# An attention-and-feed-forward kernel whose whole work becomes a list of jobs, planned into one fixed order for all five engines

## The chip, the cores and the metric

The kernel runs on one core of a Trainium2 chip. That core has a matrix engine (PE; its weight loads are listed apart as PEld), a vector engine (DVE), an activation engine (ACT), a general engine (POOL), a queue engine (SP) that issues most transfers, and 16 DMA engines that carry them out. Each engine works through its own list of instructions strictly in order, and waits at the head of that list when an operand is not there yet. The metric is the device time of one execution in microseconds (us); lower is better.

## The reference: what is computed

There are 4 batches of 8 heads with 768 rows of 64 elements. Rows may only attend to rows that fall in the same of 64 hash buckets. The attention output, with the heads side by side, is 3072 rows of 512, and goes through a feed-forward stage with 2048 hidden units and an ELU. All inputs are float32.

```
q_bits = (einsum('bhsd,dk->bhsk', q, proj) > 0);  k_bits likewise      # 6 bits each
mask   = bucket(q_bits)[:, :, :, None] == bucket(k_bits)[:, :, None, :]
scores = where(mask, (q @ k.T) / sqrt(64), -1e9)
attn   = exp(scores - max(scores));  attn = attn / (sum(attn) + 1e-9)
x      = (attn @ v) with heads side by side                             # (3072, 512)
h      = x @ w_in                                                        # (3072, 2048)
g      = where(h > 0, h, exp(min(h, 0)) - 1)
out    = g @ w_out                                                       # (3072, 512)
```

## The kernel before, in words

**Numbers.** Every float32 operand of a matrix product is split into a high and a low half-precision part after scaling by a power of two. ACT writes the high part (a scaled copy, `scaled`, L142), DVE the low part (`rest`, L151, a scalar_tensor_tensor). A product is then three products: high by high, high by low, low by high.

**Weights.** The 16 tiles of `w_in` and the 16 of `w_out` are loaded 512 KB at a time (L503), taken apart on ACT and DVE (`wdecode`, L516 to L518), and PE forms bounds of their size (L526). From these come one scale for `w_in` (`w0s`) and one for `w_out` (`w1s`), after which every tile is split in place (`wsplit`; the rows `W<-W,w0s` and `W<-W,w1s`). The ring that the raw weights land in is the same memory (`U`) that the feed-forward stage later uses for its intermediate results, so that stage begins only when all 32 tiles are decoded.

**Attention.** A pair is two heads and half of a batch's rows (384 rows per head). Each pair has six slots, one for 128 rows of one head against all 768 keys. There are 32 pairs and 192 slots. In a slot PE makes the scores (`s`, L556, four matmuls), DVE clamps them and takes the row maximum (L568, `pt<-s`), ACT takes the exponential with its sum (L584), ACT and DVE write the normalized result as two halves (`hl`), and SP issues a transposing transfer (`PT<-hl`, L599). After its sixth slot a pair's product with v runs on PE (`attend`, `av`, 36 matmuls, L607) and ACT and DVE split its result into `x`. Before a pair's slots its q and k rows are loaded, scaled, split, transposed by a transfer, and their hash bits are written beside them (`z`, L315; `zb`, L320). Each batch's v is prepared likewise.

**Feed-forward.** A chunk is the 384 rows of four pairs; there are eight. For each of 16 groups of hidden units, `first` makes `h` (12 matmuls, L636), then ACT takes the exponential (L647), POOL scales and shifts (L650), DVE combines (L651), ACT and DVE split (`U<-U,ch`), and `second` adds into the output banks `o` (9 matmuls, L672). After a chunk's last group the banks are scaled out by ACT or DVE and sent from POOL's queue (`out_dram<-W`, L686).

**What sets the order.** The program is written as a loop over slots `G`. Tables of leads in slots (`PREP`, `VPREP`, `MOE_LAGS`, `AV_LAG`) say ahead of or behind which slot each step is written, and `run_moe` writes feed-forward work between the slots in a proportion that finishes a chunk's feed-forward while the next chunk's slots run. From the slot at which the first chunk's attention is done on, PE's list is exactly as written (`tc.manual_schedule` for PE alone). On the other engines, and on PE before that slot, the framework's own scheduler sets the order by its estimate of when each instruction can run.

## Time and profile before

| what | value |
|---|---|
| median of 3 runs | 922.37 us (921.95 to 925.62) |
| the profiled execution's own time | 921.71 us |
| its span, first to last instruction | 919.9 us |
| PE busy | 824.0 us, 90% of the span |
| DVE busy | 701.2 us, 76% |
| ACT busy | 696.8 us, 76% |
| POOL busy | 127.1 us, 14% |
| mean granted clock of PE | 0.945 |

The shares are means over stages that differ. The first feed-forward matmul starts 165 us into the span. Until then the work is weights, preparation and attention; afterwards attention and feed-forward run side by side, and at the end there is feed-forward alone. A row of the profile names the line and the engine, the tile written and the tiles read, and the shapes; `x128` is a count, a busy time is followed by the mean duration of one in nanoseconds, and an idle time stands with what ended it.

### The profile page before, as it was taken

The numbers are of one execution on the slowest core, as the hardware profiler recorded it, in microseconds if no ns is written. First come the engines' busy times: TensorE is split into PE (matmuls) and PEld (weight loads), VectorE is DVE, ScalarE is ACT, GpSimd is POOL, SyncE is SP. The second block draws the span as 40 slices with busy tenths as digits, with TensorE's granted clock in tenths as the row PEclk, the third lists the DMA queues.
The fourth block names the chain that finished last, engine by engine and source line by source line (L and its number), as shares of the span: only waits on it lengthen the run. The fifth ranks groups of instructions, "written<-read, shape, count | busy, mean of one in ns | idle before, by whom it ended". The sixth has DMA issues, their size and how long they took to land.

```text
span 919.9 us, 14869 instructions
## 1 busy us (share of the span) xinstructions
PE 824.0 (90%) x5161; PEld 441.4 (48%) x5161; DVE 701.2 (76%) x1530; ACT 696.8 (76%) x1361; POOL 127.1 (14%) x179
## 2 busy tenths in 40 slices
PE   4566456999999999999999999999999999999996
PEld 2334223455545555555445555555445555555553
DVE  6999899788877777789968686889777687674332
ACT  7877889879879677888878686888687777774332
POOL 1000000011121011221111011121111012111211
PEclk9586576899999999999999999999999999999999
DMA  9798668699887857798897777886966667654000
GB/s 325 213 259 245 170 128 156 131 172 174 164 185 149 149 104 152 149 192 134 165 200 131 130 132 130 168 177 118 168 138 130 113 117 150 99 107 81 35 1 35
DMA packets 391339, 135.12 MB, mean 147 GB/s; under 512 B 368000, under 2 KB 385632, under 8 KB 391264
## 3 DMA queue, kind: packets, MB, share of 16 engines
q1 hardware_dynamic: 389184, 127.88, 69.2%
q0 software_dynamic: 1920, 6.29, 2.0%
q8 instruction: 40, 0.66, 0.3%
q14 instruction: 35, 0.29, 0.1%
q10 hardware_dynamic: 160, 0.00, 0.0%
HBM read 35.65 MB, written 6.29 MB: 46 GB/s over the span
## 4 chain that ended last, share of the span: by engine, by line
PE 41%; DVE 18%; DMA 17%; ACT 14%; issue 8%; POOL 1%; SPq 1%; POOLq 0%; DVEq 0%; ACTq 0%
PE h L636 14%; PE o L672 14%; PE s L556 6%; PE av L607 6%; DVE pt L568 5%; DMA K<-natk 4%; DVE hl L151 4%; ACT pt L584 4%; DMA O<-nat1q 3%; ACT hl L142 3%; DMA out_dram<-W 2%; DMA PT<-hl 2%; DVE vhl L151 1%; ACT U L647 1%; POOL U L650 1%
## 5 line engine op out<-in xcount | busy, mean ns | idle before, releaser
L672 PE MATMUL o<-W,U 128*128 128x512 f16 x1152 | 279.5, 379 | 3.9 <-ACT W L142 3.9
L636 PE MATMUL h<-x,W 128*128 128x384 f16 x1536 | 280.5, 327 | 2.1 <-ACT x L616 1.8
L650 POOL TENSOR_SCALAR U<-U,ch 128x384 f32<-128x384 f32 x128 | 110.3, 862 | 750.8 <-ACT U L647 511.7
L636 PEld LDWEIGHTS <-W 128*128 128x128 f16 x1536 | 147.6, 98 | 113.9 <-issue 13.1
L584 ACT ACTIVATE pt<-pt,nb,sg 128x768 f32<-128x768 f32 x192 | 195.3, 1019 | 2.2
L151 DVE SCALAR_TENSOR_TENSOR hl<-pt,r,hl 128x768 f16<-128x768 f32 x192 | 189.0, 1011 | 7.0 <-ACT hl L142 6.7
L142 ACT ACTIVATE hl<-pt,r 128x768 f16<-128x768 f32 x192 | 168.3, 924 | 23.5 <-DVE r L594 22.4
L568 DVE TENSOR_SCALAR_CACHE_REDUCE pt<-s 128x768 f32<-128x768 f32 x177 | 168.2, 950 | 21.1 <-PE s L556 20.7
L556 PE MATMUL s<-K,O 128*128 128x384 f16 x708 | 151.3, 336 | 22.5 <-DVE pt L568 20.0
L672 PEld LDWEIGHTS <-U 128*128 128x128 f16 x1152 | 110.7, 97 | 122.8 <-issue 8.5
L651 DVE SCALAR_TENSOR_TENSOR U<-h,U 128x384 f32<-128x384 f32 x128 | 70.9, 554 | 74.9 <-POOL U L650 74.9
L556 PEld LDWEIGHTS <-O 128*128 128x128 f16 (+1 forms) x768 | 74.5, 102 | 108.1 <-issue 54.7
L647 ACT ACTIVATE U<-h,ch 128x384 f32<-128x384 f32 x128 | 72.8, 569 | 65.9 <-PE h L636 65.8
L607 PE MATMUL av<-PT,vhl 128*64 128x384 f16 x1152 | 109.5, 341 | 8.4 <-DMA PT<-hl 3.9
L151 DVE SCALAR_TENSOR_TENSOR U<-U,ch 128x384 f16<-128x384 f32 x128 | 79.6, 623 | 41.2 <-ACT U L142 40.9
L142 ACT ACTIVATE U<-U,ch 128x384 f16<-128x384 f32 x128 | 77.2, 605 | 41.6 <-DVE U L651 41.4
L607 PEld LDWEIGHTS <-vhl 128*64 128x64 f16 x1152 | 75.1, 114 | 45.4 <-issue 20.7
L581 ACT ACTIVATE nb<-m,sg 128x2 f32<-128x2 f32 x96 | 27.6, 288 | 18.1 <-DVE pt L568 17.8
L584 ACT ACTIVATION_READ_ACCUMULATOR pt<-pt,nb,sg 128x1 f32 x192 | 36.0, 188 | 0.0
L208 ACT ACTIVATE nat1q<-qst 128x384 bf16<-128x384 f32 x30 | 15.4, 514 | 21.9 <-DMA O<-nat1q 20.6
L594 DVE RECIPROCAL r<-r 128x2 f32<-128x2 f32 x96 | 15.2, 159 | 19.1 <-ACT r L593 19.1
L556 PE MATMUL so<-K,O 128*128 128x384 f16 (+1 forms) x60 | 19.2, 454 | 10.0 <-DVE pt L568 9.2
(123 smaller groups left out, 583.6 us busy)
## 6 DMA issues: line engine op xcount, KB each, us to landing
U<-in_moe_w_in_dram SPq DMA_DIRECT2D x12, 512.0 KB
vf<-in_v_dram SPq DMA_DIRECT2D x16, 384.0 KB
U<-in_moe_w_out_dram SPq DMA_DIRECT2D x12, 512.0 KB
out_dram<-W POOLq DMA_DIRECT2D x24, 256.0 KB, 3.2
qst<-in_q_dram SPq DMA_DIRECT2D x30, 192.0 KB
kst<-in_k_dram SPq DMA_DIRECT2D x14, 384.0 KB
PT<-hl SPq DMA_TRANSPOSE x192
W<-in_moe_w_in_dram SPq DMA_DIRECT2D x4, 512.0 KB
```

Of the source, the lines that this page charges most:

```text
L142: nc.scalar.activation(o, x, AF.Copy, scale=s)
L151: nc.vector.scalar_tensor_tensor(o, x, s, hi, ALU.mult, ALU.subtract)
L556: nc.tensor.matmul(s_tile[:, n, :HALF], st[o][:rows, at, :], kst[kk][:rows, j * NC + n * HC : j * NC + (n + 1) * HC, :].rearrange("p a b - ...
L568: top = nc.vector.tensor_scalar(pt.rearrange("p (n e) -> p n e", n=2), s_tile[:, :, :HALF], CLAMP, None, ALU.max, ALU.max, accum_out=duo[0 ...
L581: nc.scalar.activation(nb[:, :w], m[:, :w], AF.Copy, scale=st["sg"][:, 1:2])
L584: nc.scalar.activation(pt, pt, AF.Exp, bias=nb[:, n : n + 1], scale=st["sg"][:, 0:1], accum_out=sm[:, n : n + 1])
L607: nc.tensor.matmul(av[j * D : (j + 1) * D], vt[:, j, c, vx, :], PTs[j][:, :, px, c, :], start=n == 0, stop=n == last,)
L636: nc.tensor.matmul(h, WH[:, g * KT + t, wx, fc * P : (fc + 1) * P], c["xs"][t][:, xx, :], start=n == 0, stop=n == 3 * KT - 1,)
L647: nc.scalar.activation(e, h, AF.Exp, scale=c["ch"])
L650: nc.gpsimd.tensor_scalar(e, e, c["up"], c["dn"], ALU.mult, ALU.add)
L651: nc.vector.scalar_tensor_tensor(e, h, 0.0, e, ALU.max, ALU.min)
L672: nc.tensor.matmul(o[t][:, :DO], g16[:, gx, t * P : (t + 1) * P], WH[:, NSI + 1 + f, wx, :], start=f == 0 and i == 0, stop=f == NF - 1 and ...
```

## The change

All of the work is now written down as jobs. A job names its engine, an assumed duration, a function that emits its instructions, a key, the jobs that it comes after, and tokens that it takes and gives back (one for each buffer of a ring: score banks, `PT` tiles, `x` tiles and so on). The jobs stand for the same operations on the same tiles as before: each engine's list has the same operations in the same numbers, apart from a few one-column scalings that are now made once for each batch and not once for each chunk. Nothing about tiles, buffers, shapes or transfers is altered.

`run_plan` then goes through time in its own reckoning. At each step it looks, on every engine, for the jobs whose predecessors are done and whose tokens are free, takes the one that could start first (among those within `EAGER` of it, the one with the smallest key), emits it, and books its end. Keys of attention count slot pairs; keys of feed-forward matmuls start at 1000, so that on PE attention goes ahead of feed-forward whenever both could start. On ACT, DVE and POOL the feed-forward steps have negative keys and go ahead of attention. A job may not be taken while its key is more than `AHEAD` past the furthest attention slot. The order in which the jobs were taken is the order that all five engines now get (`tc.manual_schedule` for PE, ACT, DVE, POOL and SP). The tables of leads and the framework's scheduling are gone.

```diff
-FIRST = [3, 3]
-OTHER = (3, 3)
-MOE_LAGS = (6, 6, 6)
-AV_LAG = 4
-PREP = (18, 14, 10, 5)
...
+MULTI = 1.5
+EAGER = 0.05
+AHEAD = 6.0
+HOP = 0.06
+LATE = {"PE": 0.17, "ACT": 0.1, "DVE": 0.09, "POOL": 0.1, "SP": 0.0}
+LEAD = (6.0, 5.0, 4.0, 3.0)
+W_KEY = (-1.0, 0.35, 1.0, 4.0, 0.3, 12.0, 0.5)
+S_LAG = 5
+OUT = ("ACT", "DVE", "ACT")
...
+    def run_plan():
...
+            for u, js in near.items():
+                opts = []
+                for j in js:
+                    t = max(free[u], j.ready)
+                    ok = j.key <= front + AHEAD or j.key >= 1000
+                    for name in j.take:
+                        if not tokens[name]:
+                            ok = False
+                            break
+                        t = max(t, min(tokens[name]))
+                    if ok:
+                        opts.append((t, j))
...
+                t0 = min(t for t, _ in opts)
+                t, j = min((x for x in opts if x[0] <= t0 + EAGER), key=lambda x: (x[1].key, x[0]))
+                if best is None or t < best[0]:
+                    best = (t, j)
...
+            j.start = t
+            free[j.unit] = t + us
+            j.end = t + us + LATE[j.unit]
+            if j.move is not None:
+                dma = max(dma, t + 0.1) + j.move
+                j.end = max(j.end, dma) + 1.5
+            for name in j.give:
+                tokens[name].append(j.end)
+            j.do()
...
+                s = job("PE", 0.66, scores, D0 + d + OFF["S"], after=kst["ready"] + st["ready"], behind=(last_scores,),
+                        take=(which,), give=give)
...
+            parts.append(job("PE", 1.05, attend, ka, after=landed + list(vst["ready"][p]), behind=parts[-1:],
+                             take=("av",) if n_ == 0 else (),
...
+                prev = job("PE", 0.49, first, 1000 + 2 * seq, after=[qs[n]["x"] for n in ns] + [w_ready[g * KT + t]],
+                           behind=(prev,), take=("h",) if t == 0 else (), give=give)
...
+                prev = job("PE", 0.65, second, 1000 + 2 * seq + S_LAG, after=after, behind=(prev,), give=("g",) if t == HC - 1 else ())
...
+    with tc.manual_schedule(engines={E_.PE, E_.Activation, E_.DVE, E_.Pool, E_.SP}):
+        run_plan()
```

The first place where the order can be seen is ACT's list around the first exponential of the feed-forward stage (the row `U<-h,ch`). `W<-W,w1s` is the high part of a `w_out` tile, `hl` that of a normalized slot, `pt` an exponential, `duo` or `nb`, `r` the small columns beside it, `nat1q` and `natk` the work on q rows and on k or v rows. Before:

```order
L142 ACTIVATE W<-W,w1s 128x512
L208 ACTIVATE nat1q,qx<-qst 128x384
L142 ACTIVATE hl<-pt,r 128x768 x2
L581 ACTIVATE nb<-m,sg 128x2
L142 ACTIVATE W<-W,w1s 128x512
L584 ACTIVATE pt,sm<-pt,nb,sg 128x768 x2
L616 ACTIVATE x_1529<-av 128x384
L208 ACTIVATE nat1q,qx<-qst 128x384
L142 ACTIVATE W<-W,w1s 128x512
L593 ACTIVATE r<-sm 128x2
L647 ACTIVATE U<-h,ch 128x384
```

With the change:

```order
L205 ACTIVATE W<-W,w1s 128x512
L205 ACTIVATE hl<-pt,duo 128x768
L239 ACTIVATE natk,vx<-vf 128x768
L205 ACTIVATE hl<-pt,duo 128x768
L929 ACTIVATE U<-h,ch 128x384
L239 ACTIVATE natk,kx<-kst 128x768
L785 ACTIVATE duo<-duo,sg 128x2
L239 ACTIVATE natk,kx<-kst 128x768
L792 ACTIVATE pt,duo<-pt,duo,sg 128x768
L205 ACTIVATE U<-U,ch 128x384
L929 ACTIVATE U<-h,ch 128x384
L792 ACTIVATE pt,duo<-pt,duo,sg 128x768
```

Before, 15 of the 16 `w_out` tiles are split ahead of the first feed-forward row; now 7 are, and nine come later. Of the squares of k rows six stood ahead of it, the first batch's four and two of the next batch; now the first batch's four do.

The second place is DVE's list between the 16th and the 17th feed-forward group (`U<-h,U` is one row for each group). `pt<-s` or `pt,duo<-ss` is the maximum of one attention slot. Before:

```order
L617 SCALAR_TENSOR_TENSOR x_2760<-av,x_2760 128x384
L568 TENSOR_SCALAR pt,m<-s 128x768
L693 SCALAR_TENSOR_TENSOR ch<-ve,w0e 128x1
L694 SCALAR_TENSOR_TENSOR ch<-vs,w0s 128x1
L151 SCALAR_TENSOR_TENSOR hl<-pt,r,hl 128x768 x2
L695 RECIPROCAL ch<-ch 128x1
L697 TENSOR_TENSOR ch<-ch 128x1
L568 TENSOR_SCALAR pt,m<-s 128x768
L696 TENSOR_SCALAR ch<-ch 128x1
L651 SCALAR_TENSOR_TENSOR U<-h,U 128x384
L568 TENSOR_SCALAR pt,m<-s 128x768
L151 SCALAR_TENSOR_TENSOR U<-U,ch 128x384
```

With the change:

```order
L805 RECIPROCAL duo<-duo 128x2
L769 TENSOR_SCALAR pt,duo<-ss 128x768
L402 COPY K_2606<-K_2605 64x1536
L208 SCALAR_TENSOR_TENSOR natk<-kst,ks,natk 128x12x64
L208 SCALAR_TENSOR_TENSOR hl<-pt,duo,hl 128x768
L514 COPY nat1q<-nat1q 128x6x64
L769 TENSOR_SCALAR pt,duo<-ss 128x768
L208 SCALAR_TENSOR_TENSOR hl<-pt,duo,hl 128x768
L208 SCALAR_TENSOR_TENSOR nat2q<-qst,qs,nat1q 128x6x64
L805 RECIPROCAL duo<-duo 128x2
L769 TENSOR_SCALAR pt,duo<-ss 128x768
L936 SCALAR_TENSOR_TENSOR U<-h,U 128x384
```

Between these two feed-forward groups two slot maxima stood before and four stand now (three of them in the rows shown). Counted over all engines' lists: on PE, when the feed-forward stage begins, scores of 31 slots stood ahead before and 29 do now; when its 65th group of 128 begins, 125 before and 141 now; and behind the last slot's scores there are 19 groups before and 28 now.

More of the change, by code (lines that the diff above doesn't have):

```diff
@@ L742, in lsh_attention_moe, with two @@
-    ks, qs = {}, {}
-    def prep(ns):
-        c = chunks[pairs[ns[0]][0]]
-        ps = [pairs[n][1] for n in ns]
-        b = c["b"]
+        def two():
+            nc.vector.scalar_tensor_tensor(
+                css[b][:, 4:5], vs[b]["ex"], 2.0 ** (G_DOWN - V_TOP - 2 * W_TOP), wst["e2"], ALU.mult, ALU.mult
+            )
+        key = PD * NP * 2 * b + PD * NP - 2
+        j1 = job("DVE", 0.5, one, key, after=(vs[b]["made"], w_ready["scale"][0]), take=("cs",))
+        j2 = job("DVE", 0.1, two, key, after=(j1, w_ready["scale"][1]))
@@ L768, in scale @@
-        def scale():
-            with behind_max():
-                for m in made:
-                    next(m, None)
-        def split(i):
-            for part, sts in parts:
-                part[2](sts[i], sgs[i])
-        def project(x, i):
-            part, sts = parts[x]
-            part[3](sts[i])
-        return load, sums, scale, split, project, len(parts)
-    due = []
-    last = {}
-    held = []
-    proj0 = []
-    groups = [[n] for n in range(NP)] + [[n, n + 1] for n in range(NP, len(pairs), 2)]
```

1220 lines of the change are left out of this document (617 added, 603 removed).

## The prediction

> **What bounds the kernel now.** I read the page's slices first, since the shares of the whole span mix stages.
>
> ```profile
> span 919.9 us, 14869 instructions
> PE   4566456999999999999999999999999999999996
> DVE  6999899788877777789968686889777687674332
> ACT  7877889879879677888878686888687777774332
> PEclk9586576899999999999999999999999999999999
> DMA  9798668699887857798897777886966667654000
> ```
>
> Each digit is 23 us. In the first seven PE is half idle while DVE and ACT are near full; from the eighth on PE is full and DVE and ACT have room; in the last three only PE works. The timeline of PE gives the borders: the first feed-forward matmul, and the first of the 65th of 128 groups (`h` has 12 matmuls a group).
>
> ```profile
> 164.97 1.63 PE L636 MATMUL h<-x,W 128*128 128x384 f16 x9
> ...
> 556.93 1.46 PE L636 MATMUL h<-x,W 128*128 128x384 f16 x8
> ```
>
> Busy time in the stretches between (first column pair: stretch and length; then PE, PEld, DVE, ACT, POOL busy with counts; then granted clock, share of the DMA engines, GB/s):
>
> ```profile
> 0.00:165.00 165.00, 95.96 (x561) 53.57 (x562) 145.88 (x361) 136.22 (x257) 3.00 (x27) 0.71 0.81 212
> 165.00:557.00 392.00, 379.72 (x2446) 200.94 (x2445) 314.89 (x677) 320.12 (x641) 63.65 (x73) 1.00 0.80 153
> 557.00:840.00 283.00, 276.31 (x1757) 148.81 (x1756) 218.56 (x457) 217.00 (x426) 45.85 (x56) 1.00 0.73 136
> 840.00:912.00 72.00, 72.00 (x403) 38.05 (x401) 21.14 (x36) 22.68 (x38) 12.94 (x20) 1.00 0.04 14
> 912.00:920.00 8.00, 0.02 (x1) 0.00 (x0) 0.75 (x1) 0.78 (x2) 1.67 (x3) 0.84 0.26 98
> ```
>
> So there are three different limits. Stage 1 (165 us) is DVE's: 145.9 of 165 us busy. Stages 2 and 3 (392 us, then 283 + 72 = 355 us) are PE's: it lacks 12.3, 6.7 and 0.0 us. The last 8 us are the output on its way. A gain can come from less DVE work or less DVE waiting in stage 1, or from those 19 us; PE's work itself is the same in both kernels.
>
> **Stage 1: what is put off.** Counted in the two lists, DVE has ahead of its first feed-forward row: 15 low parts of `w_out` tiles before and 7 now, 32 slot maxima before and 30 now, and one q split with its copy fewer. ACT has 8 high parts, 2 exponentials, 2 squares each of k, v and q, and one q scaling fewer. The rows by shape price them:
>
> ```profile
> L151 DVE SCALAR_TENSOR_TENSOR W<-W,w1s 128x512 f16<-128x512 f32 x16 | 11.9, 744 | 0.7 <-ACT W L142 0.6
> L568 DVE TENSOR_SCALAR_CACHE_REDUCE pt<-s 128x768 f32<-128x768 f32 x177 | 168.2, 950 | 21.1 <-PE s L556 20.7
> L151 DVE SCALAR_TENSOR_TENSOR nat2q<-qst,qs,nat1q 128x384 f16<-128x384 f32 x30 | 18.4, 613 | 5.8 <-ACT nat1q L142 5.6
> L161 DVE COPY nat1q<-nat1q 128x384 f16<-128x384 f16 x30 | 7.8, 261 | 0.0
> L142 ACT ACTIVATE W<-W,w1s 128x512 f16<-128x512 f32 x16 | 11.4, 712 | 2.0 <-DVE W L151 1.9
> L584 ACT ACTIVATE pt<-pt,nb,sg 128x768 f32<-128x768 f32 x192 | 195.3, 1019 | 2.2
> L208 ACT ACTIVATE natk<-kst 128x768 bf16<-128x768 f32 x14 | 11.7, 837 | 4.2 <-DMA kst<-in_k_dram 2.4 <-DMA K<-natk 1.8
> ```
>
> DVE: 8 x 0.744 + 2 x 0.950 + 0.613 + 0.261 = 8.7 us less. ACT: 8 x 0.712 + 2 x 1.019 + 4 x 0.837 (v taken like k) = 11.1 us, and the q rows on top; ACT does not become the limit. With DVE's waiting unchanged the feed-forward stage begins 8.7 us sooner, at 156.3. The waiting is the unknown here. The waits of DVE in stage 1:
>
> ```profile
> DVE pjx L204 <- DMA pf<-in_proj_dram: 6.2, 1, 6.2
> DVE K L304 <- PE zh L301: 3.6, 4, 1.5
> DVE W L517 <- ACT W L516: 3.4, 3, 1.7
> ```
>
> The 6.2 us at the start stand for a load that both kernels wait for. Of 19.1 us idle (165 - 145.9) at most 13 can go. In the new list the first two pairs' k and q and all of the first v are loaded ahead of the first weight tile, where before a weight tile came third; that gives DVE less to do in the first 15 us, and it can as well cost a few. The transfers set a floor that does not bind: 0.81 x 165 = 134 us of them. Bounds: 8.7 us of new waits (nothing gained) to 13 us of old ones gone. I take 3 us gone, near the lower side, since both named waits are for operations that stay: stage 1 ends at 153.
>
> **Stages 2 and 3: what moves across their border.** Attention goes ahead on PE whenever it can start, so it runs away from the feed-forward stage. In stage 2 PE's list holds 448 score matmuls where it held 376 (18 slots more), 36 `av` matmuls and 12 bit matmuls more, and the same 768 and 558 of the feed-forward. The chain of waits has the price of each bundle when nothing stands in its way:
>
> ```profile
> 173.77 0.70 PE z L315 x6
> 175.88 0.65 PE s L556 x4
> 177.18 1.94 PE o L672 x9
> 179.77 1.95 PE h L636 x12
> 182.37 3.05 PE av L607 x36
> ```
>
> Stage 2 grows by 18 x 0.65 + 3.05 + 2 x 0.70 = 16 us to 408. Stage 3 loses 16 slots, one `av` and two `z`: 10.4 + 3.1 + 1.4 = 15 us, to 340. The slots not done in stage 1 (2 x 0.65 = 1.3 us) are the difference.
>
> **Stages 2 and 3: waits.** PE's waits there, as the trace names them:
>
> ```profile
> PE s L556 <- DVE pt L568: 8.9, 12, 1.7
> PE o L672 <- ACT W L142: 3.9, 5, 1.7
> PE av L607 <- DMA PT<-hl: 2.9, 5, 0.8
> PE h L636 <- ACT x L616: 1.8, 1, 1.8
> ```
>
> Two should shrink. Between a chunk's last `av` and the first `h` that reads its `x`, PE had a single bundle of 1.9 us; priced by the bundles above it now has 24 to 57 us in chunks three to eight, so ACT and DVE have ample time to write `x`. Between a pair's last scores and its `av` PE has a median of 21 us of work, 16 before, for the transposing transfers to land. I take both waits (4.7 us) as gone. One should grow. There is one score bank in these stages, and its next scores wait for the maximum (0.95 us). Between two slots' scores PE always had at least 2.6 us of other work; now a quarter of them have 1.6 or less, the least 1.1. Whenever DVE comes late, all of PE's list behind those scores waits, feed-forward matmuls that could run included. Bounds: nothing more (the list was laid so that the maximum is just done) to 8.9 us again; I take half, 4 us. The output banks' wait (3.9) stays: still two output tiles, and 4 to 9 us of PE work between a bank's last and next use where there were 5 to 8. Net: 1 us less.
>
> **Sum.** 153.3 + 408 + 340 - 1 + 8 = 908 us of span. The profiled execution took 921.71 us with a span of 919.9, so 1.8 us lie around it, and it stands 0.7 us under the median. I predict 910 us, against 922.37.
>
> **Rivals.**
>
> *Saturation (slower).* The new list asks for more of everything at once. Between feed-forward groups 9 and 40 it has 61 slots, 48 before. A slot's transfers come to 0.80 x 392 / 94 = 3.3 us of all DMA engines (94 slots in stage 2, with their share of loads), so 61 make 204 us, while PE's own work there is 32 x 3.89 + 61 x 1.25 = 201 us (1.25: one slot's scores, a sixth of an `av`, its bits). DMA would be full for 200 us. Over stage 2 ACT rises to about 374 of 408 us and DVE to 364. What such a stretch costs PE the trace shows once for each batch:
>
> ```profile
> 180.00:260.00 80.00, 79.26 (x529) 42.31 (x528) 70.21 (x155) 68.03 (x136) 14.98 (x13) 1.00 0.81 154
> 260.00:280.00 20.00, 18.07 (x107) 9.21 (x106) 14.00 (x30) 14.40 (x32) 2.58 (x4) 1.00 1.08 226
> ```
>
> Where transfers fill their share to 1.08, PE loses 1.9 of 20 us; where DVE is 88% busy at 0.81, it loses next to nothing. If a late transfer holds up `av` or a score in PE's list and all of stage 2 loses 10% and not 3%, that is 28 us: 938 us. It decides from about 24 us lost in stage 2, twice the present 12. Against it: the row with DVE at 88% shows that a loaded DVE alone does not hurt, and the longer distance to `av` is room for late transfers.
>
> The Trainium skill, "TensorE: Matmul & The Clock Gate", section "What's actually happening", adds a reason to this rival: after an idle window of about 3.4 us PE's clock falls to half until it has been busy for as long. The trace agrees in kind: 0.71 granted in stage 1, 1.00 after, where no wait is over 1.8 us. By that rule a saturated stage would pay an estimated further 2 us for each stall that exceeds the window; the sum above goes without it.
>
> *No change.* DVE's new start costs what the deferral saves, stage 1 stays at 165: 165 + 408 + 340 - 1 + 8 + 1.8 = 922 us. For it: the loads' new order; against it: every row put off was ahead of the limit on the engine that is the limit.
>
> *Much faster.* The plan also removes most avoidable waits: 10 of DVE's 13 us in stage 1 (146) and half of PE's 19 later (-9): 146 + 408 + 340 - 9 + 8 + 1.8 = 895 us. Against it: 72 us of PE's tail are perfect already, and static orders on five engines carry any misjudged duration into all of them.
>
> **How the numbers follow.** My forecast (902 to 917 us) gets 0.46, much faster 0.18, no change 0.16, saturation 0.20. A measurement of this kernel tells about 0.5% (4.6 us) from no change. Faster: 0.46 + 0.18 = 0.64, and 0.01 of the no-change case that falls just beyond: 0.65. Same 0.15, slower 0.20. The range reaches down to the much faster case (893) and up through no change into the milder half of saturation (932); cases of both signs hold much of the chance, and the likeliest one's own range is 902 to 917.
>
> **What would show it.** Right: the first `h` matmul at about 153 us, DVE idle for under 17 us before it; the 65th group at about 561; in stage 2 DMA near 0.92, DVE near 89% and PE without more than 12 us of gaps; no wait of `h` for `x`; a longer tail with PE alone. Wrong: the first `h` at 160 us or later (the loads' order, or ACT late); waits of `s` for `pt` or of `av` for `PT` of 20 us and more in stage 2, with the DMA share at 1 (saturation); a granted clock under 1.00 after stage 1.

## The result, and the profile after

| | before | after |
|---|---|---|
| median, both timed side by side | 922.65 us (921.95 to 925.62) | 946.74 us (944.41 to 951.2) |
| the profiled execution's span | 919.9 us | 942.7 us |
| first feed-forward matmul | 165.0 us | 157.5 us |
| first `h` matmul of the 65th group | 556.9 us | 588.6 us |
| PE without work between those two | 12.3 us | 29.8 us |
| and from there to the last matmul | 6.7 us | 12.1 us |

The changed kernel is slower: 1.0261 times the time before, with a 95% interval of 1.021 to 1.0311. Busy time by stage in the changed kernel (stretch and length; then PE, PEld, DVE, ACT, POOL busy with counts; then granted clock, DMA share, GB/s), cut at the same four events as the prediction's table of before:

```profile
0.00:157.50 157.50, 97.68 (x553) 47.00 (x554) 141.61 (x339) 125.93 (x236) 3.22 (x27) 0.74 0.83 215
157.50:589.00 431.50, 401.66 (x2569) 212.75 (x2567) 361.47 (x763) 368.48 (x740) 61.70 (x73) 0.99 0.84 160
589.00:840.00 251.00, 238.85 (x1537) 128.41 (x1536) 177.68 (x356) 176.49 (x337) 38.54 (x49) 0.99 0.65 121
840.00:934.50 94.50, 94.50 (x508) 49.42 (x505) 29.26 (x50) 29.42 (x50) 17.58 (x27) 1.00 0.02 9
934.50:943.00 8.50, 0.23 (x2) 0.00 (x0) 0.38 (x1) 1.37 (x2) 1.67 (x3) 0.66 0.24 93
```

Stage 1 is 7.5 us shorter. Stage 2 is 39.5 us longer: PE works 21.9 us longer in it, of which 16 were expected to move there, and stands idle 17.5 us longer (431.5 - 401.7 against 12.3). Stage 3 with the tail of matmuls is 9.6 us shorter (345.5 against 355), 5.4 us less than the 15 us of work that left it, all of it idle time. The DMA engines are little busier in stage 2 (0.84 against 0.80), and DVE and ACT are 84% and 85% busy there. The waits of the changed kernel (us in total, times, longest):

```profile
PE ss L755 <- DVE pt L769: 35.0, 35, 5.5
DVE pt L769 <- DMA PT<-hl: 10.3, 8, 2.7
ACT hl L205 <- DMA PT<-hl: 15.1, 12, 4.4
PE av L846 <- DMA PT<-hl: 8.8, 5, 3.9
PE z L443 <- DMA O<-nat2q: 6.5, 3, 2.7
```

Three of these five name a transposing transfer that hands on `hl` as `PT`, and a fourth one of a pair's q rows. Before, DVE waited 0.4 us for a `PT` transfer and PE 1.6 us for `z`'s rows of q. The longest pieces of the chain of waits (start, us, what) say it too; before, one of the five longest was such a transfer, now four are:

```profile
370.42 6.12 DMA PT<-hl
502.78 6.48 DMA PT<-hl
568.07 9.46 DMA PT<-hl x2
707.71 6.93 DMA PT<-hl
```

What happens at the first of them is seen in the timelines of SP's queue, of DVE and of PE (start, duration, engine, line, operation; in brackets the idle time ahead and what ended it):

```profile
367.05 7.05 SPq L825 DMA_TRANSPOSE PT<-hl  x4
374.15 1.71 SPq L578 DMA_DIRECT2D vf<-in_v_dram  x1
```

```profile
373.73 0.24 DVE L514 COPY nat1q<-nat1q 128x384 f16<-128x384 f16 x1
376.66 0.96 DVE L769 TENSOR_SCALAR_CACHE_REDUCE pt<-ss 128x768 f32<-128x768 f32 x1 [2.69 <-DMA PT<-hl]
```

```profile
373.57 1.15 PE L913 MATMUL h<-x,W 128*128 128x384 f16 x6
377.68 1.44 PE L755 MATMUL ss<-K,O 128*128 128x384 f16 x4 [2.96 <-DVE pt L769]
378.91 1.16 PE L913 MATMUL h<-x,W 128*128 128x384 f16 x3
```

SP issues four transposing transfers in a row and needs 7.05 us for it; the plan books 1.3 us each (`job("SP", 1.3, turn, ...)`), 5.2 together. The chain's first row above is one of them, from 370.42 to 376.54. DVE's maximum writes a `pt` buffer and waits for it, PE's next scores wait for that maximum, and the feed-forward matmuls behind those scores wait too, although the group's first six had just run. After the pause four score matmuls take 1.44 us, where the price row of before has 0.65. So one late transfer goes through two engines' fixed lists and stops the third. Two errors of the plan meet here: the short booking of the issues, and a ring of buffers through which this maximum waits for a transfer that the plan does not connect with it (the first experiment below).

### The profile page after: what moved, and what is told of

The parts are those of the page before. It is cut to its first block, busy times and chain, and to the rows that moved or that the text cites. A ratio compares the mean times of both kernels' runs of the same rounds, so it can differ in the third digit from the quotient of the medians.

```text
span 942.7 us, 14818 instructions
## 1 busy us (share of the span) xinstructions
PE 832.9 (88%) x5161; PEld 437.6 (46%) x5161; DVE 710.4 (75%) x1506; ACT 701.7 (74%) x1361; POOL 122.7 (13%) x179
## 4 chain that ended last, share of the span: by engine, by line
PE 40%; DVE 25%; DMA 13%; ACT 12%; issue 7%; POOL 1%; SPq 1%; POOLq 0%; DVEq 0%; ACTq 0%
PE h L913 14%; PE o L961 13%; DMA PT<-hl 10%; DVE pt L769 7%; DVE hl L208 6%; PE av L846 6%; PE ss L755 5%; ACT hl L205 3%; ACT pt L792 3%; DVE W L676 2%; DVE U L936 1%; DVE W L208 1%; POOL U L933 1%; DMA vf<-in_v_dram 1%; PE z L443 1%
## 5 line engine op out<-in xcount | busy, mean ns | idle before, releaser
L208 DVE SCALAR_TENSOR_TENSOR hl<-pt,duo,hl 128x768 f16<-128x768 f32 x192 | 194.6, 1014 | 25.1 <-ACT hl L205 23.8
L205 ACT ACTIVATE hl<-pt,duo 128x768 f16<-128x768 f32 x192 | 176.9, 925 | 33.3 <-DVE duo L805 16.7
L792 ACT ACTIVATE pt<-pt,duo,sg 128x768 f32<-128x768 f32 x192 | 195.4, 1018 | 2.0
L769 DVE TENSOR_SCALAR_CACHE_REDUCE pt<-ss 128x768 f32<-128x768 f32 x180 | 170.9, 950 | 25.5 <-PE ss L755 14.2
L755 PE MATMUL ss<-K,O 128*128 128x384 f16 x720 | 156.0, 341 | 37.6 <-DVE pt L769 35.0
L785 ACT ACTIVATE duo<-duo,sg 128x2 f32<-128x2 f32 x96 | 27.7, 289 | 25.7 <-DVE pt L769 25.7
L792 ACT ACTIVATION_READ_ACCUMULATOR pt<-pt,duo,sg 128x1 f32 x192 | 36.0, 188 | 0.0
L864 DVE SCALAR_TENSOR_TENSOR x<-av,x 128x384 f16<-128x384 f32 x32 | 17.7, 554 | 21.4 <-ACT x L861 21.4
L687 PE MATMUL acc<-W 128*128 128x128 bf16 x128 | 16.6, 272 | 18.4 <-DVE W L676 18.4
L443 PE MATMUL z<-O,pjz 128*32 128x384 f16 (+1 forms) x168 | 22.2, 336 | 8.7 <-DMA O<-nat2q 6.5
```

The lines of the kernel that those rows point to most:

```text
L205: nc.scalar.activation(o, x, AF.Copy, scale=s)
L208: nc.vector.scalar_tensor_tensor(o, x, s, hi, ALU.mult, ALU.subtract)
L443: nc.tensor.matmul(t[u * QD : (u + 1) * QD], pj["z"][:rows, zi, :], flat(st[src])[:rows, u * w : (u + 1) * w], start=n == 0, stop=n == len ...
L755: nc.tensor.matmul(t[:, x, :HALF], st[o][:rows, at, :], kst[kk][:rows, j * NC + x * HC : j * NC + (x + 1) * HC, :].rearrange("p a b -> p ( ...
L769: nc.vector.tensor_scalar(pt.rearrange("p (n e) -> p n e", n=2), box["s", at % 2][:, :, :HALF], CLAMP, None, ALU.max, ALU.max, accum_out=b ...
L792: nc.scalar.activation(pt, pt, AF.Exp, bias=u[:, 2 + i : 3 + i], scale=st["sg"][:, 0:1], accum_out=u[:, 4 + i : 5 + i])
```

## The experiments

All but two are the changed kernel with one or more edits of the plan or its buffers (`e4_peonly` frees the other engines' lists, `e8_defer` is the kernel before with one edit). Ratios are to the kernel before, timed beside each. "Gaps" is the time in which PE ran no matmul between the first `h` and the 65th group, from all its matmul rows. Slots are the score slots that stand ahead of the 65th group in PE's list.

| run | edits | median us | ratio, 95% | first h | gaps | slots |
|---|---|---|---|---|---|---|
| changed | | 946.74 | 1.0261 (1.021 to 1.0311) | 157.5 | 29.8 | 141 |
| e1_rings | own rings of four | 941.17 | 1.021 (1.0192 to 1.0228) | 157.9 | 23.8 | 141 |
| e2_late | landing 3.5 us | 942.53 | 1.0212 (1.0178 to 1.0245) | 159.6 | 23.2 | 131 |
| e3_pace | scores held back | 932.94 | 1.0108 (1.0074 to 1.0142) | 159.0 | 20.0 | 129 |
| e4_peonly | only PE's list fixed | 989.57 | 1.0729 (1.069 to 1.0768) | 168.1 | 47.7 | 141 |
| e5_all | rings, landing, pace | 912.89 | 0.9878 (0.9856 to 0.99) | 160.2 | 9.8 | 129 |
| e6_allsp | those, SP's times | 908.84 | 0.9833 (0.9812 to 0.9853) | 161.4 | 9.7 | 129 |
| e7_ringpace | rings, pace | 930.41 | 1.0069 (1.0043 to 1.0095) | 159.7 | 21.4 | 129 |
| e8_defer | kernel before, `w_out` put off | 932.44 | 1.0094 (1.0069 to 1.0119) | 161.1 | 20.4 | 125 |
| e9_nopace | rings, landing | 916.77 | 0.9928 (0.9906 to 0.995) | 160.5 | 11.3 | 131 |
| e10_norings | landing, pace | 920.63 | 0.9965 (0.9944 to 0.9986) | 160.5 | 14.5 | 129 |
| e11_early | rings, SP's times, pace, landing from 120 us | 905.28 | 0.9802 (0.977 to 0.9834) | 161.4 | 7.4 | 129 |
| e12_dve | that, DVE's results later | 909.77 | 0.9852 (0.9829 to 0.9876) | 161.9 | 9.2 | 129 |
| e13_sponly | rings, SP's times | 922.06 | 0.9985 (0.9969 to 1.0) | 158.4 | 17.5 | 141 |
| e14_ptland | rings, landing for `PT` alone | 923.87 | 1.0011 (0.9998 to 1.0024) | 169.7 | 12.4 | 135 |
| e15_nopace | e11 without the pace | 907.74 | 0.9833 (0.9808 to 0.9858) | 162.2 | 7.9 | 138 |
| e16_noland | e11 with landing 1.5 us | 912.44 | 0.9887 (0.9863 to 0.9911) | 157.9 | 11.4 | 129 |
| e17_spalone | SP's times alone | 925.07 | 1.0027 (1.0013 to 1.0042) | 157.3 | 19.9 | 141 |

(The median of `e11_early` counts one execution of 4635 us, which the interval leaves out and no trace explains; the other three lie at 904.12 to 905.93 us.)

**The shared ring.** The plan counts four `pt` and four `hl` buffers as two rings. The code gives both out of one ring of eight in turn, so a maximum can be made to wait for the transfer that still reads an `hl`.

```diff
-    pp = ctx.enter_context(tc.tile_pool(name="pp", bufs=8))
+    pp = ctx.enter_context(tc.tile_pool(name="pp", bufs=4))
...
-                    hl = pp.tile([P, 2, S], F16, tag="p", name="hl")
+                    hl = pp.tile([P, 2, S], F16, tag="hl", name="hl")
```

> The changed kernel, but the exponentials (pt) and the split results (hl) get four buffers each, where they shared one ring of eight that is given out in turn. The memory is the same, the planned order too. The plan books them as two rings of four, so this makes the kernel what the plan takes it for. Ring theory (the shared ring makes DVE wait for a transposing transfer before it may write a slot maximum, and PE's scores behind it): the 10.3 us of DVE's waits of pt for PT<-hl go, PE's 42 us of gaps between 157 and 840 us fall below 30, time 930 to 937 us. Transfer theory (transfers land later than the plan has them): pt's waits go, but others grow in their place; gaps stay at 38 or more, time 943 to 947. Pace theory (too much attention for each feed-forward group): the same, 942 to 947.

941.17 us, 5.6 below the changed kernel and outside all three forecasts. The waits of `pt` for a transfer are gone from the list of waits, and in stage 2 the scores' waits for the maximum fall to 7.0 us, near the 5.5 of the kernel before. First the changed kernel from 157.5 to 589 us, then this run from 157.9 to 585:

```profile
PE ss L755 <- DVE pt L769: 15.4, 21, 3.0
PE ss L755 <- DVE pt L769: 7.0, 17, 1.2
```

ACT's waits for a transfer, which stand on `hl` itself, are longer than the 15.1 us of the changed kernel (both rows over the whole kernel, stage 1 included):

```profile
PE ss L755 <- DVE pt L769: 27.0, 32, 5.0
ACT hl L205 <- DMA PT<-hl: 19.6, 13, 5.5
```

So the shared ring is a fault, and by itself a small one: the transfers are as late as in the changed kernel, and `av` and `z` wait for them as long (8.8 and 6.5 us in both).

**The landing.** The plan takes a transfer as landed 1.5 us after its share of the DMA engines.

```diff
-                j.end = max(j.end, dma) + 1.5
+                j.end = max(j.end, dma) + 3.5
```

> The changed kernel, with one constant of its plan altered: a transfer is booked as landed 3.5 us after its data has moved, not 1.5. Everything that reads a transfer's data then stands later in the five lists, and the attention runs ahead a little less (57, 81 and 106 slots at groups 16, 32 and 48, where 55, 87 and 114 stand now); the first group has 30 slots ahead of it, not 29. Transfer theory: PE's waits of av for PT (8.8 us) and of z for O (6.5) go, and ACT's of hl for PT (15.1) shrink; gaps of PE below 25 us, time 925 to 935. Ring theory: pt's waits for PT stay at about 10 us and the time at 940 or more. Pace theory: about half of the gain that the lower pace brings, 935 to 942.

942.53 us, 4.2 below the changed kernel, a gain only just clear of the spread (four runs of the changed kernel at 944.41 to 951.2 us, four of this one at 937.13 to 943.4). The time is the one that the ring theory gave, but that theory had `pt`'s waits unchanged. `z` no longer waits for its rows, but the maximum now waits for a landed `PT` longer than the 10.3 us of the changed kernel, because the plan does not know of the shared ring:

```profile
DVE pt L769 <- DMA PT<-hl: 21.8, 18, 2.4
```

**The pace.** A score slot is not taken before the feed-forward group that three slots per two groups give it (the two lists hold the jobs of the scores and the first matmul job of each group).

```diff
+    for G, s in enumerate(score_jobs):
+        g = int((G - 29 - 4) / 1.5)
+        if g > 0:
+            group_jobs[g].users.append((s, False))
+            s.left += 1
```

> The changed kernel, with one dependency more in its plan: the scores of slot G may not be placed ahead of the start of feed-forward group (G - 33) / 1.5. That is the pace of the kernel before (12 slots for 8 groups) with four slots of lead; all else is planned as now. Slots ahead of groups 16, 32, 48, 64: 55, 81, 105, 129 (now 55, 87, 114, 141; before the change 53, 77, 101, 125). Pace theory: gaps of PE in 157 to 840 us fall from 42 to about the 19 of the kernel before, time 915 to 925. Ring theory: pt's waits for PT shrink with the density of slots but stay, 935 to 942. Transfer theory: av still stands too early for its transfers; 935 to 945.

932.94 us, 13.8 below the changed kernel, the most of the first three, and better than two of the forecasts and worse than the third; the 65th group came at 570.2 us instead of 588.6, with 129 slots ahead of it instead of 141. At this point the crowd of attention looked like the cause.

**The fixed lists.** Only PE keeps the planned list; the framework's scheduler orders the other four engines around it.

```diff
-    with tc.manual_schedule(engines={E_.PE, E_.Activation, E_.DVE, E_.Pool, E_.SP}):
+    with tc.manual_schedule(engines={E_.PE}):
```

> The changed kernel, with the planned order kept for PE alone; on ACT, DVE, POOL and SP the framework's scheduler orders the same instructions, written in the planned sequence. It knows the real rings. If the harm lies in the fixed lists of the four other engines (the plan's errors carried into ACT, DVE and SP), the time falls to 915 to 930 us. If it lies in PE's own list (scores, av and z ahead of their data, at whatever pace), the time stays at 940 to 955. Ring theory: DVE's waits of pt for PT go or shrink, since the scheduler sees them coming, but PE's list still holds scores too early: 935 to 945.

989.57 us, 43 us worse and outside all three forecasts, and the waits behind the same list of PE are longer, 31.1 us of ACT's for `PT` against 15.1:

```profile
PE ss L755 <- DVE pt L769: 38.6, 40, 3.8
ACT hl L205 <- DMA PT<-hl: 31.1, 21, 3.6
```

So fixing the lists of ACT, DVE and SP is not in itself what costs the time: given this list of PE, the plan's lists for them are better than the framework's.

**All three together.**

> The changed kernel with the three edits of the earlier runs together: four buffers each for pt and hl, 3.5 us for a transposing transfer's landing in the plan, and scores held to three slots per two feed-forward groups. Theory (the plan packs more attention into a group than transfers and buffers carry, and each edit mends another part of that): the gains of 14, 5.6 and 4.2 us add up at least in their larger parts, PE's gaps of the second stage fall from 29.8 us to 12 or less, and the kernel ends at 920 to 926 us, level with the kernel before. Rival (saturation of the vector and scalar engines in the second stage: what is cured at one wait comes back at the next): no more than the best single edit, 931 to 936 us, gaps 18 to 24 us. Second rival (a fixed order is harmful of itself): above 932 us with gaps of 15 us or more spread over small waits.

912.89 us, 33.9 below the changed kernel and 1.2% below the kernel before, where the single gains add up to 23.6. It is faster than the theory's 920 to 926 us. The rival that it would saturate falls: nothing came back at another wait. PE's gaps in stage 2 are 9.8 us, fewer than the 12.3 before.

**SP's times.** In stage 2 the trace of the changed kernel has these issues on SP's queue (duration in ns: least, median, most; first and last start):

```profile
L825 SPq DMA_TRANSPOSE PT<-hl x108: 1274/1725/3902, 156.9 to 573.0; - x108
L458 SPq DMA_DIRECT2D O<-zb x36: 722/744/977, 172.0 to 547.9; - x36
L458 SPq DMA_DIRECT2D K<-zb x32: 713/720/992, 224.8 to 439.7; - x32
```

The plan books 1.3 us for the first and 0.4 for each of the others. By the medians that is 108 x 0.425 + 36 x 0.344 + 32 x 0.320 = 69 us of queue time in one stage that the plan doesn't know of. The edit books what is seen for these three. K's transfers get 1.75 us too, where their median in stage 2 is 1.64; loads and the transfers of turned q rows keep their bookings:

```diff
-                turned = [job("SP", 1.3, turn, ky, after=(j2,), take=("K",), give=st["nat"], move=2.1)]
+                turned = [job("SP", 1.75, turn, ky, after=(j2,), take=("K",), give=st["nat"], move=2.1)]
...
-        return job("SP", 0.4 * quads, send, key, after=(c,), give=("zb",), move=0.1)
+        return job("SP", 0.72 * quads, send, key, after=(c,), give=("zb",), move=0.1)
...
-                landed.append(job("SP", 1.3, turn, D0 + d + OFF["L"], after=(l,), behind=landed[-1:],
+                landed.append(job("SP", 1.75, turn, D0 + d + OFF["L"], after=(l,), behind=landed[-1:],
```

> As the run with the three edits, and the plan also books what the queue of SP is seen to take: 1.75 us instead of 1.3 for issuing a transposing transfer of K or pt, 0.72 instead of 0.4 for sending a quad of hash bits. Theory (SP's queue is the booking that lags: the plan runs ahead of the trace by about 1 us in 10 as long as attention runs): 3 to 8 us below the run with the three edits, with fewer us of waits for landed transfers (av <- PT, z <- O). Rival (the landing time of 3.5 us and the pace already cover it, and SP has slack of a quarter of the stage): within 2 us of the run with the three edits.

908.84 us on top of the three, 4.1 below them, as the theory had it.

> Rings of four and the pace together, landing left at 1.5 us. Theory (edits add): 927 to 930 us; waits of pt for a transfer gone, av and z still waiting for transfers some 12 us together in the second stage. Rival (with the pace held the rings no longer matter, since pt's wait was already down to 1.7 us there): 932 to 934 us, the same as the pace alone.

Rings and pace without the landing: 930.41 us, near the rival's 932 to 934 and at the edge of the theory's range. With the pace held the rings are worth 2.5 us, less than the spread of the runs with the pace alone (929.69 to 935.03). So what the landing brings depends on the rings or the pace: 4 us alone, 17.5 on top of these two.

**The deferral alone, in the kernel before.** The splitting of `w_out` is put behind the latest exponential of the feed-forward stage, so that 8 and not 15 splits stand ahead of DVE's first feed-forward row.

```diff
-        scaled("w_hi", WH[:, d, 0, :], W[:, d + 1, :], s)
-        rest("w_lo", WH[:, d, 1, :], W[:, d + 1, :], s, WH[:, d, 0, :])
+        with tc.issue_after(latest_exp[-1].ins) if o and latest_exp else nullcontext():
+            scaled("w_hi", WH[:, d, 0, :], W[:, d + 1, :], s)
+            rest("w_lo", WH[:, d, 1, :], W[:, d + 1, :], s, WH[:, d, 0, :])
```

> The kernel before, with one part of the change alone: the splitting of w_out is put behind the latest exponential of the feed-forward, so that 8 of its 16 splits, instead of 15, stand ahead of the first h matmul. Theory (the put-off vector work sets the end of the first stage, as the changed kernel's first stage of 157.5 us against 165.0 says, and the second stage has room for it among its waits): the first h matmul comes 4 to 7 us earlier (158 to 161 us) and the kernel takes 916 to 919 us. Rival (the work that is put off is paid back in the second stage, where the vector engine is busy nine tenths of the time): first h matmul earlier, but the time within 2 us of before. Second rival (the first stage's end is set by w_in's low parts, not by w_out's): first h matmul unmoved at 164 to 166 us.

A miss for all three: the first `h` came 3.9 us sooner, and the kernel was 8.9 us slower. Windows of this run, and below them those of the kernel before:

```profile
161.00:260.00 99.00, 90.13 (x573) 47.22 (x572) 81.75 (x178) 79.97 (x160) 16.13 (x15) 0.97 0.78 147
260.00:360.00 100.00, 93.97 (x597) 48.93 (x596) 73.39 (x153) 75.91 (x153) 12.88 (x18) 0.98 0.74 145
360.00:568.00 208.00, 202.47 (x1314) 107.86 (x1313) 165.86 (x358) 169.01 (x340) 34.73 (x40) 1.00 0.79 152
```

```profile
165.00:260.00 95.00, 92.18 (x594) 48.75 (x593) 82.26 (x177) 81.59 (x163) 16.97 (x16) 0.98 0.82 156
260.00:360.00 100.00, 96.49 (x621) 50.74 (x620) 75.54 (x162) 79.15 (x160) 13.25 (x19) 1.00 0.76 148
360.00:557.00 197.00, 191.06 (x1234) 101.44 (x1232) 157.09 (x340) 159.38 (x321) 33.43 (x38) 1.00 0.81 154
```

From the first `h` to 360 us PE is idle 8.9 + 6.0 us, 2.8 + 3.5 before; after 360 us the two are alike (5.5 and 5.9). What was put off is paid for in the first 200 us of stage 2, in idle time of PE twice over (8.6 us against 3.9), in a kernel whose other lists were not made for it. How much of that is the splits themselves and how much the new order that the framework's scheduler makes around them, this run does not tell.

**Taking one of the three away.**

> The changed kernel with rings of four and 3.5 us of landing, but without the pace: what the three edits together lose when the pace is taken away. Theory (too much attention per feed-forward group is the main fault, the other two bookings are smaller ones): 934 to 940 us, the single gains of 5.6 and 4.2 us off 946.7, with the scores' waits for pt still above 6 us. Rival (with truthful bookings of the transfers the plan's own pace is right, and holding the scores only stood in for them): 911 to 918 us, like all three together.

> The changed kernel with 3.5 us of landing and the pace, but the shared ring of eight for pt and hl as it was. Theory (the shared ring costs by itself, since pt's write on the vector engine waits for a transfer that the plan does not see, as 21.8 us of such waits in the run with the late landing alone showed): 917 to 922 us, waits of pt for a landed transfer 5 us or more. Rival (with the pace held nothing comes round the ring early, so the rings don't matter, as between the pace alone and the pace with rings, 932.9 and 930.4 us): 911 to 915 us.

Without the pace 916.77 us, by the rival: the pace, which alone gave the most, is worth 3.9 us once rings and landing are right, while 131 slots still stand ahead of the 65th group. Without the rings 920.63 us, by the theory: `pt` still waits 10.2 us for landed transfers there. Rings and landing, 5.6 and 4.2 us alone, give 30.0 together. Each hides the other: a ring that is not as planned makes a later landing meet DVE, and a late transfer makes a clean ring wait on ACT.

**The version that beats both.** SP's times, rings, pace, and the later landing only from 120 us of the plan on; and the same with vector results taken as later.

```diff
-                j.end = max(j.end, dma) + 1.5
+                j.end = max(j.end, dma) + (1.5 if t < 120.0 else 3.5)
```

> The run with all bookings (908.8 us), but the landing is booked at 3.5 us only from 120 us of the plan on, and at 1.5 us before. Theory (3.5 us of landing puts work of the first stage later than it need be: the first h matmul came at 159.6 to 161.4 us in the runs with it, at 157.5 to 159.0 in those without): first h matmul at 157 to 159 us, the rest of the kernel as before, 904 to 907 us. Rival (the list of the first stage changes otherwise too, and what it gains is lost among other waits): within 2 us of 908.8 us.

905.28 us, 0.9802 of the kernel before, and within the theory's time, but not for its reason: the first `h` stayed at 161.4 us, and the gain on `e6_allsp` (the intervals of the two overlap) comes from stage 2, 389.1 us long against 393.6:

```profile
0.00:161.40 161.40, 99.39 (x563) 47.71 (x564) 145.65 (x348) 129.71 (x242) 3.22 (x27) 0.70 0.85 215
161.40:550.50 389.10, 381.69 (x2467) 201.39 (x2466) 332.93 (x699) 335.78 (x671) 61.68 (x73) 1.00 0.84 160
550.50:840.00 289.50, 287.62 (x1844) 152.92 (x1843) 214.90 (x432) 216.90 (x420) 44.77 (x63) 1.00 0.69 128
```

PE lacks 7.4 and 1.9 us in stages 2 and 3, at the same DMA share of 0.84 in stage 2 as in the changed kernel. No wait of `av` or `hl` for a `PT` transfer is left.

```diff
-LATE = {"PE": 0.17, "ACT": 0.1, "DVE": 0.09, "POOL": 0.1, "SP": 0.0}
+LATE = {"PE": 0.17, "ACT": 0.1, "DVE": 0.25, "POOL": 0.1, "SP": 0.0}
```

> As the run with the early landing, and the plan takes 0.25 us instead of 0.09 from the end of a vector instruction to its use. Theory (what is left of PE's gaps, 8.4 of 9.7 us in the second stage of the run with all bookings, waits for the vector engine's maximum over scores, whose result the plan expects too early): these gaps fall to 5 us or less and the time is 2 to 4 us below that of the run with the early landing. Rival (the vector engine is simply behind there, and no booking of its latency makes it faster): the same gaps, and the same time within 1.5 us.

909.77 us, worse by 4.5, which neither forecast had. Scores wait for the maximum 20.7 us in the whole kernel, against 17.9 in `e11_early`: what is left is not a booking of DVE's latency, and more slack in the plan is not by itself better.

**Which booking.** The issue times with the rings, the later landing for `PT` transfers alone with the rings, and the fastest version without the pace and with the early landing.

> Rings of four and the queue of SP booked as the trace has it (1.75 us for issuing a transposing transfer of K or pt, 0.72 for a quad of hash bits); landing left at 1.5 us, no pace. Theory (what the plan has wrong is the queue: the use of a landed pt came 3.8 to 4.2 us after its issue where nothing else was late, the plan's own booking is 3.7, and only the 1.3 us of issue is short): 915 to 922 us, like rings with the later landing (916.8). Rival (the later landing helps as slack of 2 us against everything that slips upstream, and true issue times give none): 932 to 941 us, like the rings alone (941.2).

> Rings of four, and 3.5 us of landing for the transposing transfers of pt alone; all other transfers keep 1.5 us, no pace. Theory (pt's transfers are the ones in the way, on the path scores, exponential, hl, PT, attend): 914 to 920 us, as with 3.5 us for all transfers (916.8). Rival (the loads, the hash bits and the turns of O and K count as much, the 6 us of z's waits in the changed kernel being of that kind): 925 us or more, and z's waits of 5 us and more stay.

> The fastest version (905.3 us: rings, queue of SP, landing of 3.5 us from 120 us on, pace) without the pace. Theory (with transfers booked truly the plan's own pace is fit, the pace only stood in): 903 to 907 us. Rival (the pace is worth its 4 us still, as between 916.8 us without and 912.9 with it): 908 to 912 us.

> The fastest version with 1.5 us of landing all along: rings, queue of SP and pace. Theory (true issue times carry the gain): 905 to 912 us, first h matmul at 157 to 159 us. Rival (slack of 2 us is needed): 925 to 931 us, like rings and pace (930.4), with av and z waiting for landed transfers again.

SP's times with the rings: 922.06 us, 19.1 below the rings alone, just outside the theory's 915 to 922 and far from the rival's. The landing for `PT` alone: 923.87 us, between the two; its first `h` came only at 169.7 us, so its stage 1 is not comparable, while its gaps in stage 2 fell to 12.4 us and `z`'s waits for q rows to 1.3. The fastest version without the pace: 907.74 us, on the edge between theory and rival, the pace worth 2.5 us by the medians, with intervals that overlap. With the early landing: 912.44 us, just outside the theory's 905 to 912, so the later landing is worth 7 us even with true issue times.

> The changed kernel with the queue of SP booked as the trace has it, and nothing else: the ring of eight for pt and hl stays shared, landing 1.5 us, no pace. Theory (the queue is the booking that lags by itself): with the rings it took off 19 us (941.2 to 922.1), and without them it takes off 15 to 22: 925 to 932 us. Rival (each of ring and queue holds the attention back by itself, so that one mended alone shows little, as the landing alone did with 4 us against 24 with the rings): 938 to 944 us.

SP's times alone, with shared ring, early landing and no pace: 925.07 us, 21.7 below the changed kernel, the largest of all single edits. The ring did not hide it. Its stages, then its waits:

```profile
157.30:575.80 418.50, 398.57 (x2568) 210.34 (x2567) 359.70 (x763) 366.09 (x738) 61.00 (x73) 1.00 0.84 164
575.80:840.00 264.20, 258.48 (x1656) 137.11 (x1655) 183.29 (x366) 182.07 (x348) 42.22 (x55) 1.00 0.61 115
840.00:912.90 72.90, 72.87 (x390) 37.88 (x387) 22.77 (x39) 22.79 (x38) 13.63 (x21) 1.00 0.03 12
```

```profile
PE ss L755 <- DVE pt L769: 29.5, 33, 3.3
DVE pt L769 <- DMA PT<-hl: 8.2, 7, 2.6
ACT hl L205 <- DMA PT<-hl: 6.6, 7, 2.2
PE av L846 <- DMA PT<-hl: 3.4, 3, 1.6
PE z L443 <- DMA O<-nat2q: 1.6, 3, 0.8
```

This run decides between the two readings. It packs as much attention into stage 2 as the changed kernel (141 slots ahead of the 65th group in both, the same numbers of PE, DVE and ACT instructions within three, the same DMA share), and yet its stage 2 is 13 us shorter and its stage 3 with the tail 8.4 us. So this amount of attention per group does not by itself cost the time; the order of the five lists that the plan made with its short issue times costs 21.7 us more than the order made with the measured ones. How the new order acts is shown only in part. The waits of `av`, `z` and `hl` for transfers fall by more than half, those of `pt`, which come from the shared ring, by a fifth. From the end of a slot's low part on DVE to the start of its transfer's issue it takes 4.3 us on average, 5.5 in the changed kernel and 2.1 in the kernel before (192 transfers, paired in order of time). PE's own work between a pair's last scores and its `av` did not grow (a median of 20.6 us over the 28 pairs from the first `h` on, 22.0 in the changed kernel), so it is not that `av` was put behind more of it.

## Why the prediction was wrong, point by point

I predicted 910 us (893 to 932), faster with a chance of 0.65. It is 946.74 us, outside the range and with the other sign.

**Stage 1: 153.3 predicted, 157.5 measured.** The 3 us of waits gone are right: DVE is idle 157.5 - 141.6 = 15.9 us, 19.1 before. The 8.7 us of put-off vector work are mis-sized; DVE's busy time to the first `h` fell by 4.3 (145.9 to 141.6). I had counted the splits ahead of DVE's first feed-forward row and timed the stage at PE's first `h`, which is another border. The first of these rows came 9.0 us sooner, but that it is near 8.7 is luck. Of before, and then of the changed kernel:

```profile
172.44 0.55 DVE L651 SCALAR_TENSOR_TENSOR U<-h,U 128x384 f32<-128x384 f32 x1
```

```profile
163.45 0.56 DVE L936 SCALAR_TENSOR_TENSOR U<-h,U 128x384 f32<-128x384 f32 x1 [0.40 <-POOL U L933]
```

Up to that row the counted operations are gone, and the durations of DVE's rows add up to 9.5 us less (175.7 to 166.2). DVE's busy time is only 3.85 us less there (151.01 to 147.16), since consecutive rows overlap in the trace, by 25 us in all before and 19 after; its idle time fell by the other 5.1 us. A price of count times mean duration left this overlap out. Why it shrank is open.

That put-off work is a gain for the whole was taken for granted and isn't shown by any run: where it was made alone (`e8_defer`) stage 2 took it back and more, and the two fastest versions have a first `h` at 161 and 162 us.

**Stage 2's work: 16 us more predicted.** PE's busy time grew by 21.9 us in the changed kernel and by 18.9 in `e17_spalone`, which has the same work on PE in that stage at a mean granted clock of 1.00. The price of the moved bundles was short by some 3 us, and slow clock (below) is the other 3.

**Stage 3: 15 us less predicted; with its tail 9.6 measured**, 18 in `e17_spalone`. PE's work fell by 15, to 333.4 us, as predicted. Waits took the rest.

**The waits: the step that failed.** "Net: 1 us less" was 23 us more idle time of PE in stages 2 and 3. I took `av`'s wait for `PT` as gone, since a median of 21 us of PE's work lies between a pair's last scores and its `av`; it went from 2.9 to 8.8 us. `z`'s wait for the transfer of a pair's q rows, 6.5 us, was not in the sum at all. I costed the work between on PE's side and did not follow what must happen in that time: the turn of six transfers in SP's queue, among loads, hash bits and turned q and k rows, at 1.73 us a piece. No row of SP's queue stands in the prediction. For the scores I priced one maximum on DVE (0.95 us) against the PE work between, and took 4 us more; it was 11.3 (8.9 to 20.2 over the two stages). In stage 2 most of that came from the maximum's waits for transfers through the ring that `pt` and `hl` share: with own rings (`e1_rings`) the scores wait 7.0 us there and not 15.4. I had not looked at which buffers share a ring. Right were `h`'s wait for `x`, which is gone, and that the wait of `o` for ACT would not grow; it vanished.

**Saturation, the rival that came nearest (938 us).** Its sign and its threshold held: about 24 us lost in stage 2, 29.8 measured. Its mechanism did not. It asked for the DMA engines to be full between groups 9 and 40; their share there was 0.87 (199.3 to 430.4 us), and in `e17_spalone` it is 0.88 (198.6 to 422.5 us) in a stage 2 that is 13 us shorter. Over all of stage 2 `e17_spalone` and `e11_early` work at the same 0.84 as the changed kernel, with 10 and 22 us less idle time. So the same load on the engines that carry transfers does not force the loss; what the plan lacked was the knowledge of when a transfer is issued and which buffer it holds.

**The clock.** I wrote that a saturated stage would pay about 2 us more for each long stall. The changed kernel has three stretches of 3.41 us at half clock in stages 2 and 3, after PE pauses of 2.96, 2.15 and 3.86 us, all of them waits for `PT` (the first through the maximum):

```profile
372.00:384.00 12.00, 9.04 (x49) 4.28 (x47) 8.74 (x16) 7.62 (x15) 0.79 (x1) 0.86 1.05 185
506.00:514.00 8.00, 5.85 (x41) 2.99 (x39) 3.77 (x7) 4.67 (x10) 1.60 (x2) 0.79 0.72 223
708.00:720.00 12.00, 8.14 (x56) 5.04 (x54) 6.24 (x11) 6.55 (x14) 1.85 (x4) 0.86 0.77 158
```

```profile
509.30 4.79 PE L846 MATMUL av<-PT,vhl 128*64 128x384 f16 x35 [2.15 <-DMA PT<-hl]
```

35 `av` matmuls take 4.79 us there, where 36 took 3.05 before. That pause is followed by 1.8 us of loss (4.79 - 35/36 x 3.05), and three such dips come to an estimated 5 us (half of 3 x 3.41). The rule of the Trainium skill that I had cited ("TensorE: Matmul & The Clock Gate", section "What's actually happening") speaks of idle windows of about 3.4 us; the trace agrees with its slow stretch of about as long, and shows one after a pause of 2.15 us already. The kernel before has one too, after the pause of 1.81 us behind its first `h` matmuls, which "1.00 after" in the prediction passes over: a mean over 392 us hides 3.41. On the other hand, pauses of 2.53 and 2.75 us in the changed kernel (waits of `z`, at 236 and 440 us) were followed by none. So these runs give no length of pause from which the clock falls. The kernel before at its dip, then the changed kernel after the pause of 2.75 us:

```profile
169.90:173.30 3.40, 3.40 (x13) 1.55 (x12) 2.18 (x6) 2.77 (x5) 0.66 (x1) 0.50 1.05 193
443.20:447.00 3.80, 3.76 (x24) 2.07 (x24) 2.66 (x5) 0.75 (x1) 0.00 (x0) 1.00 1.16 205
```

**Much faster and no change.** "Much faster" had the right reason against it, that static orders on five engines carry a misjudged duration into all of them. That reason should have weighed on the forecast too, since durations to be misjudged stood in the diff (1.3 and 1.5 us) beside rows that could have been compared, here SP's of before (least, median and most in ns):

```profile
L599 SPq DMA_TRANSPOSE PT<-hl x192: 1274/1727/3730, 37.5 to 837.2; - x192
```

With rings, issue times and landing mended and the pace held the design gives 905.28 us, without the pace 907.74, close to my number. That nearness is in part luck: in the version without the pace stage 1 takes 162.2 us where my sum has 153.3, and stages 2 and 3 up to the last matmul take 738.2 where it has 747.

## What to carry to other kernels

When a change replaces a scheduler by a plan with written durations, compare every written duration with its row in the trace first, those of the issuing queue above all, and check that the plan's tokens are the buffers that the code really has. A small misbooking can cost much: here booking some 0.45 us more for each transposing transfer and 0.32 for each small one gained 21.7 us. Faults of such a plan hide each other (5.6 and 4.2 us alone, 30 together), so a single edit that gains little does not clear its suspect.

## What the runs showed of the hardware that was not expected

Issuing a transposing transfer of 128 x 1536 elements kept SP's queue for 1.73 us by the median and up to 3.9 us, about as long in the kernel before (1.727) as in the changed one; a small one of 12 x 384 elements took 0.72 to 0.74. The 1.3 us of the plan are near what such a transfer takes on a queue that was idle: after 2 us and more without an issue the median is 1.43 us (1.27 to 1.47, 22 of them), directly behind another issue 1.75 (140 of them); the kernel before has 1.43 and 1.75 as well. In the idle cases the DMA engines had little to do either (a median share of 0.08 against 0.95 from 2 us ahead of the issue to its end), so what makes an issue longer is not shown. In `e5_all` and `e9_nopace`, where an `av` had to wait more than half a microsecond for `PT`, it started 3.9 to 4.6 us after that transfer's issue had begun and 0.5 to 0.7 us after its last packet (in each of the eight cases, worked out from the packets); in the changed kernel, with transfers issued back to back, it was up to 7.1 us after the issue.

What stays open: why a landing of 3.5 us still helps by 7 us when the issue times are right (`e16_noland` against `e11_early`), though the plan's earlier booking nearly meets those 3.9 us; and whether the true issue times matter as such or only as longer ones, since no run booked them longer than the trace has them. With own rings the later landing did even more (`e9_nopace`, 916.77 us) than the true issue times (`e13_sponly`, 922.06 us), so slack in some other place of the plan's transfers is not ruled out. What the runs show is that the plan's bookings of transfers and buffers made the loss, not which of them is the one to mend.
